# Eight experts on one core: weight pieces leave the branches, half of the first block's second layer goes into them, and small outputs move to a branch without matmuls

## The chip, the cores and the metric

The kernel runs on one core of one Trainium2 chip. Its engines are TensorE (PE, matmuls), VectorE (DVE), ScalarE (ACT), GpSimd (POOL) and SyncE (SP, which here only issues DMAs); each has its own instruction queue and runs it in order, and they wait for one another through semaphores. The metric is device time of the whole kernel in microseconds (us).

## The reference

Three parts follow each other. A chunked attention over 2 batches, 8 heads and 768 positions gives x of 1536 tokens by 512. A dense layer (512 to 2048 to 512, with a sigmoid gate) transforms x. Then a router takes, for each token, the best of 8 experts and gives it to that expert, up to a capacity of 384 tokens:

```
expert_idx = np.argmax(x @ w_gate, axis=1)
disp[e, counts[e]] = x[i]                      # tokens of expert e, in order
h = np.maximum(np.einsum('ecd,edf->ecf', disp, w1), 0.0)    # 512 -> 1024
y = np.einsum('ecf,efd->ecd', h, w2)                        # 1024 -> 512
out[i] = gate_w[i] * y[expert_idx[i], pos[i]]
```

The change touches the third part alone. With the inputs used, the experts have, in the order in which the kernel takes them (EORDER), 224, 291, 128, 160, 128, 256, 160 and 189 tokens. This text calls them the first to the eighth expert.

## The kernel before

Every float32 operand of a matmul is split into a high and a low part, and three products (high-high, high-low, low-high) stand for one. The tokens of an expert lie in blocks of 128. How many blocks an expert has is known only at run time, so the kernel branches on the count (tc.If, on every engine): a body of such a branch is called a leaf here.

The first layer (512 to 1024) has eight columns of 128 (fc). For one block (`first_of`) it is computed as two halves and transposed; for two blocks it is computed column by column (`first_of_two`, 12 matmuls per column); where the second block has at most 64 tokens, `first_of_narrow` computes a column with 8 matmuls, ACT and DVE make from it `low` and then `hT`, and POOL copies the second block's part of `hT` into `hp` (line 1084), two copies after all eight columns. The second layer (1024 to 512) of a block takes 24 matmuls of 512 columns (`layer2_part`, line 1003), that of a small block 16 (`small2`, line 941). Its result is scaled by the gate weight (ACT, line 1012; DVE, lines 944 and 945, for a small block) and scattered into the output by a POOL DMA (lines 1013 and 946).

Weights come as pieces, eight per expert (four of w1, four of w2), 512 KB each. SP loads a piece into one of eight raw buffers (line 241), ACT rounds it to its high part (line 295) and DVE subtracts that to get the low part (line 300). Six slots hold two pieces each. `w_next` moves the stream of pieces on by one; `steps(0)` brings it to the first three pieces of the next expert, `steps(1)` to all eight, which is possible when `w1_done` has given up the slots of the current first layer. So pieces 0 to 2 are made during the first layer of the expert before, and 3 to 7 behind it.

Before the change `steps(1)` stands inside every leaf, the second layer of the second block too, and all 24 matmuls of the first block's second layer come after the branches have met. Among these, an instruction (`hint`, lines 1191 and 1535) tells PE's sequencer which arm the next expert will probably take. The inputs take these leaves: the first expert its lone second block; the second expert two blocks and a third small one; the third and the fifth expert one block ("one"); the fourth, seventh and eighth the narrow leaf; the sixth two full blocks.

A scheduler orders the instructions of each engine within a block of the program; it doesn't move them over a branch. At the end of a leaf each engine's semaphore is brought to a common value.

## Time and profile before

| | us |
|---|---|
| median of three runs | 551.02 (548.78 to 552.99) |
| the profiled execution | 546.83 |
| its span | 545.0 |
| PE busy | 506.7 (93% of the span) |
| DVE, ACT, POOL busy | 316.3, 277.0, 117.4 |

The profiled execution lies 1.83 us above its span, and 0.8% below the median. The experts run from about 346 us to the end. A busy share is an average over the three parts; in the experts' part PE's idle times stand one by one in the timeline, each with what ended it. [...]

### The profile page before, as it was taken

The page shows a single profiled execution, that of the slowest core. Times are in us where ns is not written, and L with a number is a line of the kernel's source. Part 1 is how long each engine was busy: PE and PEld are TensorE (multiplying, and loading weights), DVE is VectorE, ACT ScalarE, POOL GpSimd, SP SyncE. Part 2 cuts the span into 40 slices and gives each one's busy share as a digit, 9 for nine tenths or more (in the row PEclk, how much of TensorE's full clock was granted, in tenths as well). Part 3 has the DMA queues.
Part 4 walks back from the last instruction along what each step waited for, and adds up shares of the span by engine and source line. Part 5 has one row for each costly group of instructions (what it writes and reads, how often), then busy time and mean ns, then how long its engine had stood idle before and what let it go on. Part 6 is the DMA issues. An engine that isn't in the chain of part 4 may idle for free.

```text
span 545.0 us, 10544 instructions
## 1 busy us (share of the span) xinstructions
PE 506.7 (93%) x4085; PEld 434.9 (80%) x4085; DVE 316.3 (58%) x633; ACT 277.0 (51%) x573; POOL 117.4 (22%) x113
## 2 busy tenths in 40 slices
PE   7899999999999999999999999978999499994985
PEld 3688889889999888999988887768887477984873
DVE  4999893687962652223373346293548918578231
ACT  2898877757632442222453334382637718666130
POOL 3335443334210220000000000630044133031201
PEclk9999999999999999999999999998999889998888
DMA  8887562043430022000285113797549938770100
GB/s 312 316 308 282 193 223 101 12 151 111 149 121 1 2 70 86 1 0 1 74 278 191 40 60 118 222 323 288 165 146 290 356 96 267 273 253 22 47 4 30
DMA packets 39163, 81.52 MB, mean 150 GB/s; under 512 B 3945, under 2 KB 10089, under 8 KB 39082
## 3 DMA queue, kind: packets, MB, share of 16 engines
q1 hardware_dynamic: 36010, 70.66, 37.5%
q0 software_dynamic: 3072, 9.80, 5.8%
q8 instruction: 48, 0.79, 0.6%
q14 instruction: 33, 0.27, 0.2%
HBM read 70.96 MB, written 9.75 MB: 148 GB/s over the span
## 4 chain that ended last, share of the span: by engine, by line
PE 70%; issue 8%; DMA 7%; DVE 6%; ACT 3%; POOL 1%; another core or an unknown queue 1%; SPq 1%; POOLq 0%; ACTq 0%; DVEq 0%
PE psh L547 25%; PE acc L590 25%; PE psy L1003 6%; DMA raw<-in_w_dram 4%; PE psh L879 3%; PE psy L941 3%; ACT w L295 3%; DVE w L300 2%; PE pse L505 2%; PE pss L435 1%; POOL hp L1084 1%; DMA kt<-in_k_dram 1%; DMA raw<-in_w_out_dram 1%; PE psr L615 1%
## 5 line engine op out<-in xcount | busy, mean ns | idle before, releaser
L547 PEld LDWEIGHTS psh<-xT,w 128*128 128x128 f32 x1152 | 147.0, 188 | 8.0 <-ACT g L566 0.3
L590 PE MATMUL acc<-w,g 128*128 128x512 f32 x576 | 153.0, 400 | 0.0
L547 PE MATMUL psh<-xT,w 128*128 128x256 f32 x1152 | 151.7, 281 | 0.0
L590 PEld LDWEIGHTS acc<-w,g 128*128 128x128 f32 x576 | 100.7, 188 | 19.4 <-issue 2.1
L562 ACT ACTIVATE sg<-psh 128x256 f32<-128x256 f32 x96 | 36.6, 383 | 126.1 <-PE psh L547 124.2
L300 DVE TENSOR_TENSOR w<-raw,w 128x1024 fp32r<-128x1024 f32 x64 | 76.4, 1221 | 28.3 <-ACT w L295 14.3
L570 DVE TENSOR_TENSOR g<-sg,g 128x256 fp32r<-128x256 f32 x78 | 38.2, 490 | 80.3 <-ACT g L566 77.7
L295 ACT ACTIVATE w<-raw 128x1024 fp32r<-128x1024 f32 x64 | 65.5, 1062 | 9.7 <-DMA raw<-in_w_dram 6.6
L1003 PE MATMUL psy<-w,hT 128*128 128x512 f32 x240 | 58.7, 398 | 0.8 <-DVE y L944 0.4
L1003 PEld LDWEIGHTS psy<-w,hT 128*128 128x128 f32 x240 | 44.4, 188 | 11.9 <-issue 1.1
L1012 ACT ACTIVATE y<-psy,gt 128x512 f32<-128x512 f32 x10 | 6.9, 689 | 60.7 <-PE psy L1003 55.9
L566 ACT ACTIVATE g<-psh 128x256 fp32r<-128x256 f32 x96 | 36.2, 379 | 0.0
L601 DVE SCALAR_TENSOR_TENSOR x<-acc,x 128x512 f32<-128x512 f32 x36 | 24.1, 686 | 20.8 <-PE acc L590 20.8
L827 POOL DMA_INDIRECT xr<-rows,taker x23 | 28.1, 1220 | 21.8 <-ACT w L295 6.8
L1069 PE MATMUL psh<-xs,w 128*128 128x384 f32 x96 | 28.8, 341 | 3.1 <-DVE low L1075 1.8
L879 PE MATMUL psh<-xs,w 128*128 128x256 f32 x192 | 25.4, 295 | 5.9 <-DVE w L300 3.2
L941 PE MATMUL psy<-w,hp 128*128 128x512 f32 x48 | 16.7, 520 | 15.2 <-POOL hp L1084 15.2
L879 PEld LDWEIGHTS psh<-xs,w 128*128 128x128 f32 x192 | 24.8, 201 | 6.9 <-issue 3.6
L725 POOL DMA_INDIRECT y<-rows,taker x1 | 1.2, 1213 | 123.8 <-DVE cnt_i L732 123.8
L941 PEld LDWEIGHTS psy<-w,hp 128*128 128x128 f32 x48 | 12.4, 264 | 19.0 <-POOL hp L1084 15.9
L1071 PE MATMUL psh<-xs,w 128*128 128x256 f32 x96 | 26.9, 280 | 0.0
L300 POOL TENSOR_TENSOR w<-w,w 128x512 fp32r<-128x512 f32 x12 | 16.7, 1400 | 42.8 <-ACT w L295 42.8
(163 smaller groups left out, 678.5 us busy)
## 6 DMA issues: line engine op xcount, KB each, us to landing
raw<-in_w_dram SPq DMA_DIRECT2D x64, 512.0 KB, 6.8
raw<-in_w_out_dram SPq DMA_DIRECT2D x16, 512.0 KB, 4.4
raw<-in_w_in_dram SPq DMA_DIRECT2D x16, 512.0 KB, 5.1
vt<-in_v_dram SPq DMA_DIRECT2D x12, 512.0 KB
kt<-in_k_dram SPq DMA_DIRECT2D x12, 368.0 KB, 5.3
qt<-in_q_dram SPq DMA_DIRECT2D x12, 256.0 KB, 6.2
out_dram<-blank SPq DMA_DIRECT2D x12, 256.0 KB, 2.6
rows<-x SPq DMA_DIRECT2D x5, 520.0 KB
```

Source lines behind the costliest of these rows:

```text
L295: nc.scalar.activation(out=w_dst(self.name, self.i, 0), in_=w, func=AF.Copy)
L300: eng.tensor_tensor(out=lo, in0=w, in1=hi.bitcast(F32), op=ALU.subtract)
L547: nc.tensor.matmul(ps, lhsT=w[:, wz, c, i * P:(i + 1) * P], rhs=xT[tb][:, xz, c, :], start=n == 0, stop=n == 3 * KC - 1)
L562: nc.scalar.activation(out=sg_t[u], in_=h_t[u], func=AF.Silu, scale=1.702)
L566: g_last[:1] = [nc.scalar.activation(out=g[:, 0], in_=h_t.pop(u), func=AF.Silu, scale=1.702).ins]
L570: lo = eng.tensor_tensor(out=g[:, 1], in0=sg_t.pop(u), in1=g[:, 0].bitcast(F32), op=ALU.subtract)
L590: nc.tensor.matmul(acc_t[tb][s], lhsT=g[:, gz, s * P:(s + 1) * P], rhs=w[:, wz, wi, :], start=i == 0 and n == 0, stop=u == last_of(k, tb) ...
L827: return nc.gpsimd.indirect_dma_start(out=t, out_offset=None, in_=rows[:, :], in_offset=bass.IndirectOffsetOnAxis(ap=taker[:, b, ex:ex + 1 ...
L879: mm = nc.tensor.matmul(ps, lhsT=w[:, wz, c, f0:f0 + P], rhs=t[:, xz, c, :], start=m == 0, stop=m == 3 * KC - 1)
L941: nc.tensor.matmul(ps, lhsT=h[:, fc].rearrange("p z n -> p (z n)"), rhs=w[:, wz, fc % 4, :], start=fc == 0 and wz == 0, stop=fc == F2 - 1 ...
L1003: nc.tensor.matmul(ps, lhsT=h[:, hz, fc, o:o + P], rhs=w[:, wz, fc % 4, :], start=fc == 0 and n == 0, stop=fc == F2 - 1 and n == 2)
L1069: nc.tensor.matmul(ps[:, :2 * n].rearrange("p (z n) -> p z n", z=2), lhsT=w[:, 0, c, f0:f0 + P], rhs=t[:, :, c, :n], start=c == 0, stop=False)
```

## The change

Inside the leaves no weight piece of the stream beyond `steps(0)` is left. Each leaf now ends with the first 12 matmuls (columns 0 to 3) of the first block's second layer (`head(0)`), behind the whole second layer of a second block. After the branches have met come `w1_done`, the other 12 matmuls (`tail(0)`), `steps(1)` and the gate; then a new branch on the count, which holds the scaling and the scatter of the second block (`send_second`) and no matmuls; then the first block's output. In the narrow leaf POOL copies into `hp` column by column, and the stream is moved once within the leaf (PUMPS_N) rather than three times. The hints are gone. The first expert has the same form with its blocks exchanged.

```diff
--- before.py
+++ after.py
@@ -33,6 +33,7 @@
 FROM = 150
 EV1 = 2
 PUMPS = (1, 3, 5)
+PUMPS_N = (4,)
 RAWS = 4
 RT = (4, 7)
 LOADS = 1000
@@ -41,7 +42,7 @@
 KEEP = 4
 KEEPS = (3, 8, 8)
 HALF = P // 2
-HEAD2 = 2
+HEAD2 = 4
 PUMPS1 = (0, 1, 1, 0)
 GFC = 2
 EORDER = (1, 2, 0, 3, 4, 5, 6, 7)
@@ -907,8 +908,6 @@
                 pv = ps[:, :KC * HALF].rearrange("p (c n) -> p c n", n=HALF)
                 nc.scalar.activation(out=x[:, :, 0], in_=pv, func=AF.Copy)
                 nc.vector.tensor_tensor(out=x[:, :, 1], in0=pv, in1=x[:, :, 0].bitcast(F32), op=ALU.subtract)
-                if e == 0:
-                    start2()
                 hs = []
                 for j in range(2):
                     w_tile(("w1", e, j), 0)
@@ -940,6 +939,9 @@
                 for wz in range(2):
                     nc.tensor.matmul(ps, lhsT=h[:, fc].rearrange("p z n -> p (z n)"), rhs=w[:, wz, fc % 4, :],
                                      start=fc == 0 and wz == 0, stop=fc == F2 - 1 and wz == 1)
+
+        def send_small(b):
+            ps = y_of(b)
             y = ep.tile([P, DM], F32, tag="y", name="y", bufs=2)[:HALF]
             nc.vector.tensor_scalar(out=y, in0=ps[HALF:], scalar1=gt[b][:HALF], scalar2=None, op0=ALU.mult)
             nc.vector.scalar_tensor_tensor(out=y, in0=ps[:HALF], scalar=gt[b][:HALF], in1=y, op0=ALU.mult, op1=ALU.add)
@@ -1002,10 +1004,6 @@
                 for n, (hz, wz) in enumerate(((0, 0), (0, 1), (1, 0))):
                     nc.tensor.matmul(ps, lhsT=h[:, hz, fc, o:o + P], rhs=w[:, wz, fc % 4, :],
                                      start=fc == 0 and n == 0, stop=fc == F2 - 1 and n == 2)
-
-        def layer2(b):
-            layer2_part(b, y_of(b), range(HEAD2 if e == 0 and b == 1 else 0, F2))
-            send(b)
 
         def send(b):
             y = ep.tile([P, DM], F32, tag="y", name="y", bufs=2)
@@ -1078,18 +1076,17 @@
                                                op0=ALU.max, op1=ALU.subtract)
                 if fc == TFC:
                     after_mm = mm.ins
-                if fc in PUMPS:
+                nc.gpsimd.tensor_copy(hT["pair"][:, fc], h[:, :, fc, P:n])
+                if fc in PUMPS_N:
                     w_next(e, KEEPS[0])
-            for z in range(2):
-                nc.gpsimd.tensor_copy(hT["pair"][:, :, z], hT_of(0)[:, z, :, P:P + HALF])
             with tc.issue_after(after_mm):
                 next_trans()
             steps(0)
 
-        def both(cond, yes, no, label=None):
+        def both(cond, yes, no):
 
             before = w_state()
-            with tc.If(cond, label=label) as some:
+            with tc.If(cond) as some:
                 yes()
             after = w_state()
             w_back(before)
@@ -1097,102 +1094,73 @@
                 no()
             assert w_state() == after
 
-        def start2():
-
-            layer2_part(1, y_of(1), range(HEAD2))
-
         def w1_done():
             for j in range(F // 512):
                 w_free(("w1", e, j))
 
-        def second_first():
-
-            w1_done()
-            steps(1)
-            layer2_part(1, y_of(1), range(HEAD2, F2 - 4))
-            parts[1].hint()
-            layer2_part(1, y_of(1), range(F2 - 4, F2))
-            send(1)
-
-        def third_first(b):
-
-            def go(is_wide):
-                if is_wide:
-                    trans(b, "h")
-                    start2()
-                    block_h(b)()
-                else:
-                    small_h(b)
-                second_first()
-                second_of(b, is_wide)
-
-            both(cnt[ex] > b * P + HALF, lambda: go(True), lambda: go(False))
-
-        def lone_second():
-            start2()
-            second_first()
-
-        def second_of(b, wide):
-
-            gate(b)
-            if wide:
-                layer2(b)
-            else:
-                small2(b)
-
-        def big():
-
-            both(cnt[ex] < P + HALF + 1, narrow_arm, wide)
-
-        def narrow_arm():
-
-            first_of_narrow()
-            w1_done()
-            steps(1)
-            second_of(1, False)
-
-        def wide():
-
-            first_of_two()
-            both(cnt[ex] < 2 * P + 1, two, third)
-
-        def two():
-
-            w1_done()
-            steps(1)
-            second_of(1, True)
-
-        def one():
-
-            first_of(0)
-            w1_done()
-            steps(1)
-
-        def third():
-
-            for b in range(2, NCB):
-                both(cnt[ex] > b * P + HALF, lambda: third_of(b, True), lambda: third_of(b, False))
-
-        def third_of(b, is_wide):
+        def head(b):
+
+            layer2_part(b, y_of(b), range(HEAD2))
+
+        def tail(b):
+
+            layer2_part(b, y_of(b), range(HEAD2, F2))
+
+        def third_first(b, is_wide):
 
             if is_wide:
                 trans(b, "h")
                 block_h(b)()
             else:
                 small_h(b)
-            two()
-            second_of(b, is_wide)
-
-        def hint():
-
-            traced = nc.cur_bb.bb.instructions
-            n = len(traced)
-            last = [i for i in traced if i.engine == mybir.EngineType.PE][-1].name
-            tc.mark_branch_hint_location(f"arms{e}", hint=cnt[ex] > P, engines=[mybir.EngineType.PE])
-            for i in traced[n:]:
-                tc.add_manual_dep(
-                    i, last, mybir.DependencyInfo(mybir.DependencyClass.NoSync, mybir.DependencyReason.DATA),
-                    reason="hint")
+
+        def third_second(b, is_wide):
+
+            gate(b)
+            if is_wide:
+                layer2_part(b, y_of(b), range(F2))
+                send(b)
+            else:
+                small2(b)
+                send_small(b)
+
+        def third(b, then):
+
+            def go(is_wide):
+                third_first(b, is_wide)
+                ys.pop(b, None)
+                third_second(b, is_wide)
+                then()
+
+            both(cnt[ex] > b * P + HALF, lambda: go(True), lambda: go(False))
+
+        def one():
+
+            first_of(0)
+            head(0)
+
+        def narrow_two():
+
+            first_of_narrow()
+            small2(1)
+            head(0)
+
+        def wide_two():
+
+            def then():
+                layer2_part(1, y_of(1), range(F2))
+                head(0)
+
+            first_of_two()
+            both(cnt[ex] < 2 * P + 1, then, lambda: third(2, then))
+
+        def send_second(wide):
+
+            gate(1)
+            if wide:
+                send(1)
+            else:
+                send_small(1)
 
         def after_first():
 
@@ -1212,25 +1180,31 @@
             y_of(1)
             hT_of(2)
             xs_of(2)
-            both(cnt[ex] < 2 * P + 1, lone_second, lambda: third_first(2))
+            both(cnt[ex] < 2 * P + 1, lambda: head(1), lambda: third(2, lambda: head(1)))
+            w1_done()
+            steps(1)
+            tail(1)
+            send(1)
 
         def others():
 
             assert NCB == 3
-            y_of(1)
+            for b in range(2):
+                y_of(b)
             for b in range(2, NCB):
                 load(b)
                 hT_of(b)
                 xs_of(b)
-            both(cnt[ex] > P, big, one, label=f"arms{e}")
+            both(cnt[ex] > P, lambda: both(cnt[ex] < P + HALF + 1, narrow_two, wide_two), one)
+            w1_done()
+            tail(0)
+            steps(1)
             gate(0)
-            layer2_part(0, y_of(0), range(1))
-            if e + 1 < E:
-                parts[e + 1].hint()
-            layer2_part(0, y_of(0), range(1, F2))
+            with tc.If(cnt[ex] > P):
+                both(cnt[ex] > P + HALF, lambda: send_second(True), lambda: send_second(False))
             send(0)
 
-        return SimpleNamespace(hint=hint, adopt=adopt, load=load, trans=trans, xs_of=xs_of, after_first=after_first, others=others,
+        return SimpleNamespace(adopt=adopt, load=load, trans=trans, xs_of=xs_of, after_first=after_first, others=others,
                                before_arms=before_arms)
```

How this moves instructions is shown at three places. SP at the end of the first expert's leaf (the lone second block) and behind it; raw_0_3362 to raw_3_3365 and raw_0_4523 to raw_3_4526 are the eight raw buffers. Before:

```order
L1092 COMPARE_AND_BRANCH
L241 DMA raw_3_3365<-in_w_dram 128x2x512
L241 DMA raw_0_4523<-in_w_dram 128x2x512
L241 DMA raw_1_4524<-in_w_dram 128x2x512
L241 DMA raw_2_4525<-in_w_dram 128x2x512
L241 DMA raw_3_4526<-in_w_dram 128x2x512
L1092 UNCONDITIONAL_BRANCH
```

(where the leaves have met, one load of raw_2_3364 follows, ahead of the second expert's arms). Now:

```order
L1089 UNCONDITIONAL_BRANCH x2
L242 DMA raw_2_3364<-in_w_dram 128x2x512
L242 DMA raw_0_4523<-in_w_dram 128x2x512
L242 DMA raw_1_4524<-in_w_dram 128x2x512
L242 DMA raw_2_4525<-in_w_dram 128x2x512
L242 DMA raw_3_4526<-in_w_dram 128x2x512
L242 DMA raw_3_3365<-in_w_dram 128x2x512
L1089 COMPARE_AND_BRANCH x2
```

The leaf has no load any more; raw_2_3364 is loaded first behind it, ahead of the five others.

PE in the fourth expert, the end of the narrow leaf (psy is the sum of a second layer, hp the second block's first-layer result, hT that of the first block, w_95 and w_1723 the slots of w2), and its meeting point. Before:

```order
L846 MATMUL pst<-ident,xr 128x128 x8
L941 MATMUL psy<-w_95,hp 128x512 x8
L941 MATMUL psy<-w_1723,hp 128x512 x8
L1092 UNCONDITIONAL_BRANCH
...
L1003 MATMUL psy<-w_95,hT 128x512 x3
L1191 REGISTER_ALU
L1535 BRANCH_PREFETCH_HINT
L1003 MATMUL psy<-w_95,hT 128x512 x9
L1003 MATMUL psy<-w_1723,hT 128x512 x12
L1092 COMPARE_AND_BRANCH x2
```

Now:

```order
L847 MATMUL pst<-ident,xr 128x128 x8
L940 MATMUL psy<-w_95,hp 128x512 x8
L940 MATMUL psy<-w_1723,hp 128x512 x8
L1005 MATMUL psy<-w_95,hT 128x512 x12
L1089 UNCONDITIONAL_BRANCH
...
L1005 MATMUL psy<-w_1723,hT 128x512
L1203 COMPARE_AND_BRANCH
L1089 COMPARE_AND_BRANCH
L1089 UNCONDITIONAL_BRANCH x2
L1203 UNCONDITIONAL_BRANCH
L1005 MATMUL psy<-w_1723,hT 128x512 x11
L1089 COMPARE_AND_BRANCH x2
```

Twelve of the 24 matmuls now stand in the leaf; one matmul, the new branch and eleven matmuls stand behind it, and the hint is gone.

DVE from the end of the third expert's leaf ("one") into the fourth expert's narrow leaf; each L300 or L301 row makes the low part of one piece, the slots w_95, w_1723, w_96 and w_4519 say which. Before:

```order
L300 TENSOR_TENSOR w_95<-raw_1_4524,w_95 128x1024
L300 TENSOR_TENSOR w_1723<-raw_2_4525,w_1723 128x1024
L300 TENSOR_TENSOR w_1723<-raw_3_4526,w_1723 128x1024
L1092 UNCONDITIONAL_BRANCH
L858 TENSOR_SCALAR gs<-gs 128x1
L859 RECIPROCAL gt<-gs 128x1
L1092 COMPARE_AND_BRANCH x2
L300 TENSOR_TENSOR w_94<-raw_0_3362,w_94 128x1024
L300 TENSOR_TENSOR w_94<-raw_1_3363,w_94 128x1024
L1075 TENSOR_TENSOR low<-psh,low 128x192 x2
```

Now:

```order
L1089 UNCONDITIONAL_BRANCH
L301 TENSOR_TENSOR w_95<-raw_0_4523,w_95 128x1024
L301 TENSOR_TENSOR w_95<-raw_1_4524,w_95 128x1024
L301 TENSOR_TENSOR w_1723<-raw_2_4525,w_1723 128x1024
L301 TENSOR_TENSOR w_1723<-raw_3_4526,w_1723 128x1024
...
L1203 UNCONDITIONAL_BRANCH
L301 TENSOR_TENSOR w_4519<-raw_3_3365,w_4519 128x1024
L1089 COMPARE_AND_BRANCH x2
L301 TENSOR_TENSOR w_94<-raw_0_3362,w_94 128x1024
L301 TENSOR_TENSOR w_94<-raw_1_3363,w_94 128x1024
L1073 TENSOR_TENSOR low<-psh,low 128x192 x2
```

Five pieces have left the leaf: four stand where the leaves have met, ahead of the new branch, and the piece left over from the next expert's w1 stands behind it; so seven pieces lie between the leaf's end and the first `low` of the fourth expert, where two were.

## Rows read from the trace of the kernel before

**Rows 1.** The page, busy time of the engines:

```profile
PE 506.7 (93%) x4085; PEld 434.9 (80%) x4085; DVE 316.3 (58%) x633; ACT 277.0 (51%) x573; POOL 117.4 (22%) x113
```

**Rows 2.** PE, timeline of the second expert: start, us, work, [idle before, releaser]:

```profile
366.45 8.88 PE L879 MATMUL psh<-xs,w 128*128 128x256 f32 x60 [3.20 <-DVE w L300]
377.00 4.60 PE L879 MATMUL psh<-xs,w 128*128 128x256 f32 x36 [1.67 <-DVE hT L883]
```

**Rows 3.** Stretches: length, busy us of each engine (instructions), granted clock, DMA share, GB/s:

```profile
366.45:381.44 14.99, 13.32 (x96) 13.12 (x97) 5.95 (x10) 3.42 (x9) 1.90 (x1) 0.89 0.81 285
502.95:508.72 5.77, 5.77 (x16) 4.59 (x17) 0.00 (x0) 0.00 (x0) 0.00 (x0) 0.63 0.03 6
526.64:532.00 5.36, 5.36 (x16) 4.25 (x17) 0.00 (x0) 0.00 (x0) 0.00 (x0) 0.68 0.03 6
368.00:370.00 2.00, 2.00 (x12) 2.00 (x11) 1.00 (x2) 0.38 (x1) 0.35 (x1) 0.50 0.96 332
```

**Rows 4.** DVE, timeline ahead of the second expert's start:

```profile
359.41 9.16 DVE L300 TENSOR_TENSOR w<-raw,w 128x1024 fp32r<-128x1024 f32 x8
```

**Rows 5.** The chain of waits into the second expert, its last step:

```profile
366.92 8.22 DMA raw<-in_w_dram
```

**Rows 6.** PE, timeline of the sixth expert (both layers):

```profile
461.85 11.67 PE L879 MATMUL psh<-xs,w 128*128 128x256 f32 x95 [1.06 <-DVE gs L858]
474.15 11.32 PE L1003 MATMUL psy<-w,hT 128*128 128x512 f32 x48
```

**Rows 7.** PE, timeline of the third and fourth expert:

```profile
394.13 3.90 PE L941 MATMUL psy<-w,hT 128*128 128x512 f32 x16
...
403.47 1.79 PE L963 MATMUL psh<-w,xs 128*128 128x512 f32 x7
...
417.96 0.41 PE L1069 MATMUL psh<-xs,w 128*128 128x384 f32 x1 [1.29 <-DVE gs L858]
...
426.44 0.45 PE L1069 MATMUL psh<-xs,w 128*128 128x384 f32 x1 [1.05 <-DVE low L1075]
...
436.14 5.27 PE L941 MATMUL psy<-w,hp 128*128 128x512 f32 x16 [6.26 <-POOL hp L1084]
441.77 5.85 PE L1003 MATMUL psy<-w,hT 128*128 128x512 f32 x24 [0.35 <-issue]
```

**Rows 8.** DVE, timeline: the third expert's last pieces, the fourth's last columns:

```profile
413.19 4.62 DVE L300 TENSOR_TENSOR w<-raw,w 128x1024 fp32r<-128x1024 f32 x4
...
433.45 1.03 DVE L1077 SCALAR_TENSOR_TENSOR hT<-low,hT 128x192 fp32r<-128x192 f32 x2
```

**Rows 9.** POOL, timeline, the fourth expert's second copy into hp:

```profile
434.54 1.54 POOL L1084 CAST hp<-hT 128x512 fp32r<-128x512 f32 x1 [0.28 <-DVE hT L1077]
```

**Rows 10.** PE, timeline of the seventh and eighth expert:

```profile
493.25 0.44 PE L1069 MATMUL psh<-xs,w 128*128 128x384 f32 x1 [0.77 <-DVE low L1075]
...
502.95 5.93 PE L941 MATMUL psy<-w,hp 128*128 128x512 f32 x16 [6.25 <-POOL hp L1084]
...
526.64 5.54 PE L941 MATMUL psy<-w,hp 128*128 128x512 f32 x16 [2.68 <-POOL hp L1084]
...
533.02 5.69 PE L1003 MATMUL psy<-w,hT 128*128 128x512 f32 x22 [0.38 <-DVE y L944]
```

**Rows 11.** DVE, timeline, the eighth expert's last column and its second block's output:

```profile
525.20 0.36 DVE L1077 SCALAR_TENSOR_TENSOR hT<-low,hT 128x192 fp32r<-128x192 f32 x1 [0.43 <-ACT hT L1076]
532.22 0.75 DVE L944 TENSOR_SCALAR y<-psy,gt 64x512 f32<-64x512 f32 x1 [6.66 <-PE psy L941]
```

**Rows 12.** The chain that ended last, a step of its end:

```profile
534.02 2.83 DMA out_dram<-y,taker
```

**Rows 13.** The page: ACT's half of a piece; weight loads; one instruction queue:

```profile
L295 ACT ACTIVATE w<-raw 128x1024 fp32r<-128x1024 f32 x64 | 65.5, 1062 | 9.7 <-DMA raw<-in_w_dram 6.6
...
raw<-in_w_dram SPq DMA_DIRECT2D x64, 512.0 KB, 6.8
...
q8 instruction: 48, 0.79, 0.6%
```

## The prediction, made before the changed kernel ran

> **What bounds the kernel now.** I read the page first, then PE's timeline through the experts, then the chain of waits where PE stands idle. PE is busy for 93% of the span [rows 1], so the experts are worth reading gap by gap: only an idle time of PE, or a stretch in which PE runs slowly, can be won. Five places count. The second expert starts after 3.20 us of idle time that ended with a DVE weight piece [rows 2]: DVE was still making the pieces of the first expert's leaf, eight in 9.16 us [rows 4], and PE needs none of the last five. The same expert's first layer takes 14.99 us at a mean clock of 0.89, with 0.50 early in it [rows 3] and a stall of 1.67 [rows 2]; the sixth expert's, of the same shape, takes 11.67 [rows 6]. The narrow leaves wait 6.26, 6.25 and 2.68 us for POOL's `hp` copies [rows 7, 10]. Their 16 small matmuls then run slowly: 5.27, 5.77 and 5.36 us [rows 7, 3], where the same 16 took 3.90 in the second expert [rows 7], because the clock in these stretches was 0.63 and 0.68 [rows 3], after idle times of 6.25 and 2.68. Small gaps stand at three meeting points: 1.29 and 1.06 behind DVE's gate, 0.35 and 0.38 behind the leaf [rows 7, 6, 10].
>
> **The change, part by part.** Times are us against the profiled 546.83.
>
> Second expert. The five pieces leave the first expert's leaf, so the 3.20 goes. The load of raw_2 was issued at 366.92 and took 8.22 [rows 5], behind those five loads on SP; now it waits only for its own buffer, which DVE finishes five pieces earlier, 5 x 1.15 = 5.7 us [rows 4], so near 361. It then lands near 369, about when PE has run through its free sums (five columns of 11.67 / 8 = 1.46). So the first layer should take the sixth expert's time: 14.99 - 11.67 = 3.32 saved. I take off 1.1 for what is late next, the fifth column's wait and fewer filling matmuls in the small third block (bounds 0 and 3.3). **-5.4.**
>
> Third expert ("one"). PE reaches the end of the leaf after half the second layer. 24 matmuls are 24 x 0.236 = 5.7 us (11.32 / 48, [rows 6]); PE ended at 417.96 - 1.29 = 416.67, so the half ends at 413.8. DVE ends the leaf's last piece at 413.19 + 1.15 = 414.35 [rows 8]. The meeting point joins both: **+0.55.**
>
> Fourth expert (narrow). The 1.29 goes, since the gate no longer follows the last piece. But seven pieces now stand ahead of its first `low` on DVE where two did. PE starts it near 417.4 (414.35, twelve matmuls 2.8, branches 0.2) and comes to its fifth column, which needs the first sum's bank back, 4 x 1.24 later, at 422.4 (six columns lie between 417.96 and the wait at 426.44, [rows 7]). DVE needs until 414.35 + 7 x 1.15 = 422.4 for the pieces alone, and the gate and `low` come on top: a gap of under 1 at the least. Where DVE also waits once or twice for ACT's halves (1.06 each) or for a load (6.8 from its issue, [rows 13]), it is up to 3. I take 2.0, against 1.05 before [rows 7]: +0.95. The clock stayed up after 1.29 idle and fell after 2.68, so I charge half of 1.4: +0.7. The copies per column leave only the last of eight behind the last `hT`. It costs about 0.4 (a quarter of 1.54, [rows 9]) and lies beside the first small matmuls, which need the earlier columns; in the eighth expert the last `hT` ended at 525.56 [rows 11], 1.6 after PE's first layer, and the seven pairs of matmuls ahead of it take 3.4. So the 6.26 goes, and with it 5.27 - 3.90 = 1.37 and 0.35; +0.2 for a first copy that is late. -1.29 + 0.95 + 0.7 - 6.26 - 1.37 - 0.35 + 0.2 = **-7.4.**
>
> Fifth and sixth expert: the same join, +0.55; the 1.06 goes; the same backlog, but a wide column takes 0.22 more than a narrow one, four of them 0.9, so a gap of 1.1: **+0.6.**
>
> Seventh expert: 6.25 goes, 5.77 - 3.90 = 1.87 of slow clock too; pieces 3, 0 and 1 ahead of the first `low` give a gap of 1.1 for 0.77 [rows 10], +0.2 for the copy: **-7.6.** The long leaf of the sixth expert hides pieces 4 to 7; without that cover it would be the second rival.
>
> Eighth expert: 2.68, 5.36 - 3.90 = 1.46 and 0.38 go; no pieces follow: **-4.5.**
>
> End. The first block's scatter must follow the second's, which takes 2.83 after its issue [rows 12]. Before, the second's was out at 534.02, near five us ahead of PE's end. Now its two DVE steps (0.75 each, [rows 11]) follow the leaf, whose end lies 2.8 ahead of PE's end: 2.8 cover all but 1.5 of 1.5 + 2.83, and the first block's own scaling half of that. **+0.8** (0 to 2).
>
> Branches. Behind one matmul PE meets the new branch, at seven experts. The trace shows 0 (row 474.15 follows a branch without a gap, [rows 6]) to 0.35 and 0.38 for a meeting point [rows 7, 10]; I take 0.2, nearer the middle as more jumps stand here: **+1.4** (0 to 2.7). [...] No row here times a branch alone. The hints are gone: at the two experts that take the "one" leaf, the farthest jump, 0.4 each by the 0.38, **+0.8** (0 to 2 x 6.8, the nearest DMA row from above).
>
> Removing the pieces' stream steps from the narrow columns (two of three) costs nothing: the same pieces are made later, and counted above.
>
> Sum: -5.4 + 0.55 - 7.4 + 0.6 - 7.6 - 4.5 + 0.8 + 1.4 + 0.8 = -20.8, so 526.0 for the profiled execution. The median of the runs lies 0.77% above it (551.02 / 546.83), so 530.
>
> **Rivals.** First, slower: **PE waits for its instructions.** The far jumps, leaf to meeting point and meeting point to the next arms, lose their hint and have 12 and 11 matmuls in front, 2.8 and 2.6 us of cover. Instructions do come by DMA (48 transfers on one queue, [rows 13]); a DMA took from 2.83 [rows 12] to 6.8 [rows 13] here. With 2.83 the cover holds; with 5.0 it lacks 2.2 and 2.4, 4.6 per expert, 32 over seven: 546.83 - 20.8 + 32 = 558, 562 as a median. It decides from about 4.7 us: then it eats 20.8 and 5.5 more. Against it: unhinted leaf ends before cost 0.35, 0.38 or nothing, though with 16 or 24 matmuls ahead of them. [...] 6%.
>
> Second, **the pieces start only where the leaves meet for every engine**, as PE before waited for DVE's leaf end [rows 2]. Then pieces 4 to 7 aren't hidden by the leaves of the fourth, sixth and seventh expert either. With four pieces (4.6), the gate, the branch and three or one more pieces behind the leaf's end, the waits inside the fifth, seventh and eighth expert grow by 1.2, 2.0 and 1.5, the slow clock returns in two of them (1.4 each), and the full gap of 3 stays in the fourth and sixth (1.0 and 1.0): +9.5, 535.5, a median of 540. 20%.
>
> Third, better: **the backlog is hidden and the jumps cost nothing.** Without 0.95, 0.7, 1.1, 0.33, 2.2, 0.8: 6.1 less, 520, a median of 524. 13%.
>
> Fourth, the gains are found but are given back to loads: the experts from the second to the fourth draw 285 to 332 GB/s at DMA shares of 0.81 to 0.96 [rows 3], and a stream that starts later in each expert can't catch up. If each of the first three gives back its 4 to 5 us, 14 in all: 540, a median of 544; with more, no change. 6%.
>
> **How the numbers follow.** My forecast has 55%. A change of 1%, 5.5 us, is about what a measurement of this kernel tells from none. Forecast and third rival, most of the second and half of the fourth lie below 545.5: 0.86 faster; 0.08 within 1%; 0.06 slower. The range goes from the third rival with the lowest of the runs' spread (524 - 2) to the second and the fourth: 522 to 544.
>
> **What would show it.** Right: no idle time at the second expert's start, none or under 1 us ahead of the small matmuls of the narrow leaves, these at 3.9 us, and waits of 1 to 3 us for `low` at the fifth column of the fourth, sixth and seventh experts. Wrong: idle time of PE's sequencer at the jumps (the chain would say issue or PEq), or a granted clock under 0.8 in the new leaves.

## The result and the profile after

The changed kernel takes 531.43 us (median of four runs, 530.1 to 537.04) against 551.06 beside it: a ratio of 0.9665, with a 95% interval of 0.9586 to 0.9743. Forecast were 530, and 522 to 544. The profiled execution has 531.93 us and a span of 530.1, 14.9 less than before.

PE's timeline through the experts, in the order of the second to the eighth; columns as in [rows 2]:

```profile
364.67 11.69 PE L880 MATMUL psh<-xs,w 128*128 128x256 f32 x96 [0.82 <-DVE w L301]
...
403.47 0.51 PE L965 MATMUL psh<-w,xs 128*128 128x512 f32 x1 [0.90 <-issue]
...
420.73 0.59 PE L1067 MATMUL psh<-xs,w 128*128 128x384 f32 x1 [3.45 <-DVE low L1073]
...
427.80 3.98 PE L940 MATMUL psy<-w,hp 128*128 128x512 f32 x16
...
431.62 5.76 PE L1005 MATMUL psy<-w,hT 128*128 128x512 f32 x24
...
441.74 5.79 PE L965 MATMUL psh<-w,xs 128*128 128x512 f32 x18 [4.36 <-issue]
...
456.08 5.86 PE L880 MATMUL psh<-xs,w 128*128 128x256 f32 x48
...
464.35 7.48 PE L880 MATMUL psh<-xs,w 128*128 128x256 f32 x48 [2.40 <-DVE hT L884]
...
489.59 0.45 PE L1067 MATMUL psh<-xs,w 128*128 128x384 f32 x1 [0.98 <-DVE low L1073]
...
495.35 3.98 PE L940 MATMUL psy<-w,hp 128*128 128x512 f32 x16
...
518.00 5.73 PE L1005 MATMUL psy<-w,hT 128*128 128x512 f32 x24
```

The second expert starts after 0.82 us of idle time where [rows 2] had 3.20, and its first layer runs through in 11.69, the sixth expert's 11.67 of [rows 6]. The small matmuls of the narrow leaves (L940) follow without a wait and take 3.98 where [rows 7, 10] had 5.27 and 5.93 behind 6.26 and 6.25. Three waits are new or longer. The fifth column of the fourth expert waits 3.45 for `low` (1.05 before, [rows 7]), that of the sixth 2.40, and ahead of the fifth expert PE stands idle for 4.36 us with nothing that the profile shows to wait for; 18 matmuls behind it take 5.79 where 18 x 0.236 would be 4.25. The sixth expert's last four columns take 7.48 behind their wait, its first four 5.86.

Stretches of the same kernel, columns as in [rows 3]:

```profile
364.67:376.36 11.69, 11.69 (x98) 11.69 (x99) 8.76 (x13) 6.46 (x12) 2.01 (x1) 1.00 1.03 368
...
420.73:427.01 6.28, 6.28 (x33) 6.28 (x33) 4.83 (x13) 3.65 (x12) 1.71 (x6) 0.73 1.03 387
...
427.80:431.62 3.82, 3.82 (x19) 3.09 (x18) 3.41 (x6) 3.82 (x8) 1.12 (x3) 1.00 0.11 36
...
437.38:441.74 4.36, 0.00 (x1) 0.04 (x1) 1.23 (x1) 1.63 (x2) 1.94 (x2) 0.95 1.02 366
```

Granted clocks are shares of full speed; the traces of both kernels have only 1.00 and 0.50, and a value between them is a mean over a stretch. The second expert's first layer has the full clock (1.00), the fourth expert's last four columns behind the wait of 3.45 have 0.73, the small matmuls 1.00. The sixth expert's last four columns have 0.77, the 18 matmuls behind the idle 4.36 us 0.74. In the idle time of 4.36 the DMA engines are full: share 1.02, 366 GB/s.

By segments, from one expert's first matmul to the next one's, worked out from the two timelines:

| expert | before | after | difference | forecast |
|---|---|---|---|---|
| up to the second's start, second | 16.80 + 37.02 | 14.42 + 33.71 | -5.7 | -5.4 |
| third and fourth | 43.98 | 43.36 | -0.6 | -6.9 |
| fifth and sixth | 37.85 | 42.11 | +4.3 | +0.6 |
| seventh | 29.01 | 20.95 | -8.1 | -7.6 |
| eighth | 24.40 | 18.93 | -5.5 | -4.5 |
| end | 6.29 | 6.37 | +0.1 | +0.8 |

The forecast's branches and hints (+2.2) lie across the rows. The profiles begin the experts at slightly different times (after: 0.6 later), which belongs to nothing in the change.

### The profile page after: what moved, and what is told of

The parts are those of the page before. It is cut to its first block, busy times and chain, and to the rows that moved or that the text cites. A ratio compares the mean times of both kernels' runs of the same rounds, so it can differ in the third digit from the quotient of the medians.

```text
span 530.1 us, 10682 instructions
## 1 busy us (share of the span) xinstructions
PE 503.4 (95%) x4081; PEld 435.3 (82%) x4085; DVE 317.6 (60%) x633; ACT 279.3 (53%) x573; POOL 125.3 (24%) x131
## 5 line engine op out<-in xcount | busy, mean ns | idle before, releaser
L301 DVE TENSOR_TENSOR w<-raw,w 128x1024 fp32r<-128x1024 f32 x64 | 75.5, 1221 | 29.7 <-ACT w L296 27.2
L828 POOL DMA_INDIRECT xr<-rows,taker x23 | 33.6, 1463 | 39.9 <-PE psy L1005 15.2
L1067 PE MATMUL psh<-xs,w 128*128 128x384 f32 x96 | 30.1, 352 | 4.4 <-DVE low L1073 4.4
L301 POOL TENSOR_TENSOR w<-w,w 128x512 fp32r<-128x512 f32 x12 | 16.7, 1400 | 42.7 <-ACT w L296 42.7
L291 POOL TENSOR_TENSOR w<-w,rest 128x512 int32<-128x512 int32 x13 | 17.6, 1355 | 35.4 <-DVE w L277 29.2
L965 PE MATMUL psh<-w,xs 128*128 128x512 f32 x72 | 20.1, 427 | 6.2 <-issue 5.3
L266 ACT ACTIVATE w<-raw 128x512 f32<-128x512 f32 x32 | 21.3, 675 | 8.1 <-DMA raw<-in_w_out_dram 6.6
```

The lines of the kernel that those rows point to most:

```text
L301: eng.tensor_tensor(out=lo, in0=w, in1=hi.bitcast(F32), op=ALU.subtract)
L828: return nc.gpsimd.indirect_dma_start(out=t, out_offset=None, in_=rows[:, :], in_offset=bass.IndirectOffsetOnAxis(ap=taker[:, b, ex:ex + 1 ...
L965: nc.tensor.matmul(p1[j], lhsT=x[:, xz, c, o:o + P], rhs=w[:, wz, c, :], start=(xz, wz, c) == (0, 0, 0), stop=(xz, wz, c) == (1, 0, KC - 1))
L1067: nc.tensor.matmul(ps[:, :2 * n].rearrange("p (z n) -> p z n", z=2), lhsT=w[:, 0, c, f0:f0 + P], rhs=t[:, :, c, :n], start=c == 0, stop=False)
```

## The experiments

Times are medians; the kernel before took 549.3 to 550.4 beside them, and the changed kernel, run again beside the last three, 533.07 (ratio 0.9713, 0.9665 to 0.976). Of that second run stood on record:

> The changed kernel itself, run beside the next three so that they can be compared with it: 531 by either theory, 0.966 of before.

### What the idle 4.36 us are

**The hints put back** (behind the first column, three matmuls, after the meeting point, in the changed kernel):

```diff
-            tail(0)
+            layer2_part(0, y_of(0), range(HEAD2, HEAD2 + 1))
+            parts[e + 1].hint()
+            layer2_part(0, y_of(0), range(HEAD2 + 1, F2))
```

> The changed kernel with the hints put back behind the first matmul after each meeting point; nothing else. Theory A (PE waits for the instructions of the far arm, which the removed hint would have fetched): the 4.36 us of idle time ahead of the fifth expert and the 0.90 inside the third go, and with the first the slow clock behind it (18 matmuls in 5.79 us for 4.36): 5 to 7 us less than the changed kernel, about 525. Theory B (PE waits there for something that the profile doesn't show, a semaphore or a load): the gap stays and the time is within 1 us of 531.4.

539.19 us, ratio 0.9796 (0.9746 to 0.9845). PE ahead of the fifth expert:

```profile
447.26 5.97 PE L965 MATMUL psh<-w,xs 128*128 128x512 f32 x18 [4.64 <-issue]
```

The stall stays, so theory A's expectation fell; but theory B, no change, did not hold either, since the time rose by 6 to 8 us in small waits at other places. PE's sequencer runs ahead of its matmuls (by 2.84 us at the branch shown below): by the trace this hint stood only 0.15 us ahead of its branch (439.63 and 439.78), in the kernel before 1.40 us (441.89 and 443.29). That the hints gained anything there is not shown.

**The leaf for one block first:**

```diff
-            both(cnt[ex] > P, lambda: both(cnt[ex] < P + HALF + 1, narrow_two, wide_two), one)
+            both(cnt[ex] < P + 1, one, lambda: both(cnt[ex] < P + HALF + 1, narrow_two, wide_two))
```

> The changed kernel with the outer branch turned round: the leaf for one block stands first, behind it the narrow and the wide ones; no instruction of a leaf changes. Theory A (the 4.36 us of idle time ahead of the fifth expert and the 0.90 inside the third are PE waiting for the instructions of the leaf that stood last, a long jump away): both go, with them the slow clock behind the first, 5 to 7 us less than the changed kernel, about 525; the narrow and wide leaves begin after a short jump and wait under 1 us. Theory B (every taken jump costs a fetch, the distance doesn't matter): the stall moves to the fourth, sixth, seventh and eighth expert and the time rises, 535 to 545. Theory C (PE waits for something else): no change, 531.

530.33 us, ratio 0.9654 (0.9629 to 0.968). PE:

```profile
371.48 4.77 PE L880 MATMUL psh<-xs,w 128*128 128x256 f32 x38 [2.83 <-issue]
...
424.64 0.45 PE L1067 MATMUL psh<-xs,w 128*128 128x384 f32 x1 [0.96 <-DVE low L1073]
...
440.01 4.35 PE L965 MATMUL psh<-w,xs 128*128 128x512 f32 x18
...
457.57 2.79 PE L880 MATMUL psh<-xs,w 128*128 128x256 f32 x16 [2.94 <-ACT w L296]
```

The order of leaves alone takes the stall away: the fifth expert starts at 440.01 behind the fourth's last matmul, and its 18 matmuls take 4.35. A stall of 2.83 appears in the second expert's wide leaf, which now lies farther off, two columns into it. So the idle time belongs to the place of the instructions, as A says, and it is partly moved, as B says. The 2.94 ahead of the sixth expert, and a wait of 2.16 in the third, are put down to ACT by the profile; but PE's own branch ended after ACT's piece at both (457.41 after 457.27, 414.48 after 414.42), so they are moved stalls too. The DMA queues in the 4.36 us of the changed kernel (columns: packets, MB, share of the 16 engines):

```profile
q1 hardware_dynamic: 569, 1.08, 66.7%
q0 software_dynamic: 159, 0.47, 31.8%
q14 instruction: 3, 0.02, 1.8%
q8 instruction: 1, 0.02, 1.5%
```

The profile calls q8 and q14 instruction queues; their four packets, 0.04 MB, came here among 1.1 MB of weight pieces and 0.5 MB of gathered and scattered rows. What PE did meanwhile stands in the row of its own branch (PEldq is PE's sequencer; shortest, median and longest in ns, then the start):

```profile
L1089 PEldq COMPARE_BRANCH  x1: 7030/7030/7030, 434.5 to 434.5; - x1
```

The branch to the fifth expert's leaf begins at 434.54 and takes 7.03. PE is still busy for 2.84 of it with the matmuls in its queue, and the next matmul starts 0.17 behind the branch's end: 7.03 - 2.84 + 0.17 = 4.36. So the whole stall is PE's own jump, and no other engine holds it. In the fourteen runs 100 of PE's branches from 345 us on take over 1.5 us, and in each a 16 KB packet of q8 landed 1.2 to 2.5 us ahead of the branch's end, which points to q8 as the queue that brings PE's instructions. The 0.90 inside the third expert and the 2.83 above stand behind no branch; there too a packet of q8 landed 1.6 us ahead of the next instruction.

**Half the matmuls at the leaf's end:**

```diff
-HEAD2 = 4
+HEAD2 = 2
```

> The changed kernel with HEAD2 = 2: 6 of the first block's 24 matmuls at the end of a leaf and 18 behind the meeting point, in place of 12 and 12. Theory A (queued matmuls hide the fetch behind a jump): the stall ahead of the fifth expert shrinks by the six matmuls, 1.4 us, from 4.36 to about 3, while stalls of 1 to 2 us show at the narrow leaves' ends, whose cover falls from 2.8 to 1.4 us: in all 0 to 6 us more. Theory B (the stall isn't a fetch): both stay, within 1 us of 531.4.

535.57 us, ratio 0.975 (0.9714 to 0.9785). PE at the fourth expert's meeting point and ahead of the fifth:

```profile
434.28 0.49 PE L1005 MATMUL psy<-w,hT 128*128 128x512 f32 x1 [0.74 <-ACT w L296]
...
443.36 6.54 PE L965 MATMUL psh<-w,xs 128*128 128x512 f32 x18 [4.17 <-issue]
```

The total went as A expected, the places did not: the stall ahead of the fifth expert shrank by 0.2, not 1.4, though six more matmuls stood before it, and the narrow leaves' ends cost 0.6 to 0.9 each. The six did cover 1.3 more (4.14 for 2.84), but the branch itself took 8.14 for 7.03.

### What the parts of the change are worth

**Copies by column alone** (with one step of the weight stream in the narrow leaf for three), in the kernel before:

```diff
-                if fc in PUMPS:
+                nc.gpsimd.tensor_copy(hT["pair"][:, fc], h[:, :, fc, P:n])
+                if fc in PUMPS_N:
                     w_next(e, KEEPS[0])
-            for z in range(2):
-                nc.gpsimd.tensor_copy(hT["pair"][:, :, z], hT_of(0)[:, z, :, P:P + HALF])
```

> The kernel before with one part of the change: POOL copies column by column and one step of the weight stream in a narrow leaf. Theory A (the waits for hp come from POOL's two copies after all columns): the waits of 6.26, 6.25 and 2.68 fall to 1 to 2 us and the small matmuls' clock recovers: 12 to 15 us less than before, about 537. Theory B (they come from the weight pieces which the leaf lets into the columns' chain on ACT and DVE): the first two waits stay above 4 us, only the eighth expert's goes: 4 to 7 us less.

549.7 us, ratio 0.9992 (0.9955 to 1.0029): nothing. PE in the fourth expert:

```profile
436.16 0.73 PE L942 MATMUL psy<-w,hp 128*128 128x512 f32 x2 [1.17 <-POOL hp L1082]
...
437.39 0.73 PE L942 MATMUL psy<-w,hp 128*128 128x512 f32 x2 [0.50 <-POOL hp L1082]
...
440.99 7.23 PE L1004 MATMUL psy<-w,hT 128*128 128x512 f32 x24 [2.87 <-issue]
```

The wait for hp shrinks to 1.17 and 0.50, as A said. But behind the leaf's last small matmul PE now stands idle for 2.87, and the 24 matmuls after it take 7.23 for 5.85. The same comes at the seventh (2.83) and the eighth (1.71). PE's branch at the end of this leaf, here and in the kernel before:

```profile
L1092 PEldq COMPARE_BRANCH  x1: 3550/3550/3550, 437.4 to 437.4; - x1
...
L1092 PEldq COMPARE_BRANCH  x1: 5496/5496/5496, 436.2 to 436.2; - x1
```

The jump was there before too, and longer. It began when the old wait of 6.26 was over, with all 16 small matmuls still to run: they covered 5.20 of its 5.50, and 0.35 of idle time showed. With copies by column the small matmuls run as their columns come, and when the sequencer reaches the branch PE has 0.73 left to do.

**Pieces 3 to 7 out of the leaves alone**, in the kernel before:

```diff
             first_of_narrow()
-            w1_done()
-            steps(1)
...
             both(cnt[ex] > P, big, one, label=f"arms{e}")
+            w1_done()
+            steps(1)
             gate(0)
```

> The kernel before with one part of the change: pieces 3 to 7 move from the leaves to behind the meeting point; second layers, outputs and hints stay. Theory A (the pieces in the leaf cost the 3.20 at the second expert and, in the narrow leaves, all of the hp wait above the eighth expert's 2.68): second expert 5.4 less, narrow leaves 3.5 less twice: about 10 to 12 us less than before. Theory B (pieces 4 to 7 now stand behind the second block's output, which DVE makes after the small second layer, so the next expert's columns wait): what is gained in the leaf is lost at the next expert, 3 to 6 us less or nothing.

551.61 us, ratio 1.0047 (1.0015 to 1.0078): no gain. PE in the third and fourth experts:

```profile
411.84 0.66 PE L846 MATMUL pst<-ident,xr 128*128 128x128 f32 x4 [4.06 <-DMA xr<-rows,taker]
...
427.16 0.45 PE L1069 MATMUL psh<-xs,w 128*128 128x384 f32 x1 [2.48 <-DVE low L1075]
...
435.93 4.38 PE L941 MATMUL psy<-w,hp 128*128 128x512 f32 x11 [2.84 <-POOL hp L1084]
```

The hp wait falls to 2.84, the column wait rises to 2.48 as theory B said. The third expert waits 4.06 for its rows, a gather that both theories had missed.

**The pieces back in the leaves of the changed kernel** (the first expert's stay out):

```diff
             first_of_narrow()
+            w1_done()
+            steps(1)
             small2(1)
```

> The changed kernel with the weight pieces 3 to 7 put back into the leaves of all experts but the first; copies by column, the matmuls at the leaf's end and the new branch stay. Theory A (the fetch behind the jump is slow since the loads that SP issues at the meeting point fill the DMA engines, share 1.02): with the loads in the leaf the stall ahead of the fifth expert falls below 1.5 us, the waits for the fifth column fall to those of before (about 1), and the hp waits come back at 1 to 2 us in two narrow leaves: 526 to 533. Theory B (the pieces in the leaf are what cost the time in the narrow leaves): 538 to 545.

533.8 us, ratio 0.9695 (0.9648 to 0.9743). PE at the fourth expert's meeting point and the fifth's start:

```profile
435.85 0.49 PE L1005 MATMUL psy<-w,hT 128*128 128x512 f32 x1 [2.23 <-issue]
...
441.60 4.42 PE L965 MATMUL psh<-w,xs 128*128 128x512 f32 x18 [1.10 <-issue]
```

No difference from the changed kernel that this can tell: the stall ahead of the fifth expert fell to 1.10, as A expected, but 2.23 came behind the leaf, and 1.81 behind the seventh's.

**The second block's output back in its leaf:**

```diff
             small2(1)
+            send_second(False)
             head(0)
...
-            with tc.If(cnt[ex] > P):
-                both(cnt[ex] > P + HALF, lambda: send_second(True), lambda: send_second(False))
```

> The changed kernel without the new branch: the second block's gate, scaling and scatter stand in its leaf, between its second layer and the first block's 12 matmuls. Theory A (the new branch frees DVE: in the leaf its scaling waits for the small second layer, and pieces 4 to 7 queue behind it): the fifth, seventh and eighth experts wait 1 to 3 us longer in all, some 2 to 6 us more than the changed kernel. Theory B (the branch itself costs PE 0.2 us at seven experts, and DVE has time): 1 to 2 us less.

534.37 us, ratio 0.9723 (0.9687 to 0.9758). PE:

```profile
423.57 0.69 PE L1067 MATMUL psh<-xs,w 128*128 128x384 f32 x1 [3.32 <-DVE low L1073]
...
441.57 4.43 PE L965 MATMUL psh<-w,xs 128*128 128x512 f32 x18 [1.47 <-issue]
...
491.33 0.44 PE L1067 MATMUL psh<-xs,w 128*128 128x384 f32 x1 [2.57 <-DVE low L1073]
```

The seventh expert's column waits 2.57 for 0.98, as A said; against that the stall ahead of the fifth expert is 1.47 for 4.36. Two waits for gathered rows came besides, 1.83 and 2.33. In all not to be told from the changed kernel.

**Both of these together:** pieces and outputs in the leaves, so that of the change the column copies, the missing hints, the first expert's pieces and the 12 matmuls at the leaf's end are left.

> The changed kernel with pieces 3 to 7 back in the leaves (but the first expert's) and the second block's output too, so that only the column copies, the missing hints and the 12 matmuls at the leaf's end are left of the change. Theory A (those 12 matmuls give the gain, since they hide the fetch behind the leaf's jump, which cost 2.87 and 2.83 us and a slow clock in the run with the copies alone): 535 to 540. Theory B (pieces and outputs must leave the leaf too, or PE waits for DVE at the meeting point): 541 to 549.

527.99 us, ratio 0.961 (0.9574 to 0.9646), the fastest of all, some 5 below the changed kernel beside it. PE, from the second expert to the fifth's start:

```profile
365.27 11.69 PE L880 MATMUL psh<-xs,w 128*128 128x256 f32 x96 [0.40 <-DVE w L301]
...
413.24 0.41 PE L1067 MATMUL psh<-xs,w 128*128 128x384 f32 x1 [1.27 <-DVE gs L859]
...
421.42 0.45 PE L1067 MATMUL psh<-xs,w 128*128 128x384 f32 x1 [0.75 <-DVE low L1073]
...
434.18 4.61 PE L1005 MATMUL psy<-w,hT 128*128 128x512 f32 x12 [1.96 <-issue]
...
439.44 4.42 PE L965 MATMUL psh<-w,xs 128*128 128x512 f32 x18 [0.65 <-PE psy L1005]
```

The column wait is 0.75, the fifth expert starts after 0.65, and behind the narrow leaf 1.96 are left. Theory A held, with more than it expected. Against the copies alone (549.7) that is 22 us; 5 to 6 of them are the second expert's (0.40 and 11.69 here, 3.20 and a slow clock there). The 12 matmuls were not run by themselves; that most of the rest is theirs follows from the jumps that they cover, not from a run of its own.

**The jump to the fifth expert in all these kernels.** Each row is read from PE's branch and the stretch that it takes:

| kernel | branch, us | PE busy in it | DMA share in it | idle time |
|---|---|---|---|---|
| before | 3.47 | 3.47 | 0.18 | 0 |
| changed | 7.03 | 2.84 | 0.96 | 4.36 |
| hints put back | 7.31 | 2.84 | 0.96 | 4.64 |
| half the matmuls at the leaf's end | 8.14 | 4.14 | 0.97 | 4.17 |
| pieces back in the leaves | 4.85 | 3.92 | 0.33 | 1.10 |
| output back in its leaf | 4.69 | 3.39 | 0.48 | 1.47 |
| both | 5.03 | 4.55 | 0.58 | 0.65 |

The idle time is what PE's queued matmuls leave of the branch. The branch is long where the DMA engines are full; since these kernels differ in more than their loads, that the loads lengthen it is likely, not shown.

### The wait for the fifth column

Timelines of the changed kernel between the third and the fourth expert, ACT first, then DVE:

```profile
415.24 0.69 ACT L1010 ACTIVATE y<-psy,gt 128x512 f32<-128x512 f32 x1 [2.32 <-DVEq L1203]
...
415.83 2.94 ACT L296 ACTIVATE w<-raw 128x1024 fp32r<-128x1024 f32 x3
```

```profile
409.02 5.79 DVE L301 TENSOR_TENSOR w<-raw,w 128x1024 fp32r<-128x1024 f32 x5
...
416.91 3.50 DVE L301 TENSOR_TENSOR w<-raw,w 128x1024 fp32r<-128x1024 f32 x3 [1.83 <-ACT w L296]
```

PE ended the third expert near 412.4, but ACT could scale its output only at 415.24, when DVE had made its five pieces (409.02 to 414.8) and, behind them, the gate that ACT scales by (414.92); three pieces on both engines follow, then `low`. Two kernels move this. **The output ahead of the new branch, behind an early gate:**

```diff
-            steps(1)
             gate(0)
+            steps(1)
+            if e + 1 < E:
+                send(0)
             with tc.If(cnt[ex] > P):
```

> The changed kernel with the gate ahead of the weight pieces and the first block's output ahead of the new branch (in all experts but the last). Theory A (the 3.45 and 2.40 us waits for the fifth column arise since ACT's output of the first block waits for DVE behind pieces 4 to 7, and three pieces queue behind that output): the output moves to PE's end, 412.4 in place of 415.2, DVE becomes the limit, the waits fall to about 2.0 and 1.0 and the clock in the fourth expert stays up: 3 to 6 us less. Theory B (DVE's seven pieces alone set the wait, the output's place is hidden): the waits stay within 0.5 us and so does the time.

536.95 us, ratio 0.977 (0.9708 to 0.9831), slower than the changed kernel. PE:

```profile
403.06 7.12 PE L965 MATMUL psh<-w,xs 128*128 128x512 f32 x18 [3.25 <-issue]
...
425.48 0.45 PE L1067 MATMUL psh<-xs,w 128*128 128x384 f32 x1 [1.99 <-DVE low L1073]
...
468.14 2.05 PE L880 MATMUL psh<-xs,w 128*128 128x256 f32 x15 [1.09 <-DVE hT L884]
```

The two waits fell to 1.99 and 1.09, as A expected to a tenth. The time was lost where neither theory looked: the third expert now starts after a stall of 3.25 at its jump (PE's branch takes 6.90 for 4.31), 18 matmuls take 7.12, and the seventh expert's wait rises from 0.98 to 2.95. With the leaf for one block first as well:

> The leaf for one block first (as in the run of that name) and the first block's output ahead of the new branch with an early gate. Theory A (with the long jump gone, the earlier output can now show its gain, which in its own run was lost to a longer fetch in the third expert): the waits of 0.96 in the fourth and 2.94 in the sixth expert fall to 0 to 1, 2 to 4 us less than 530.3. Theory B (the waits behind the meeting points are now set by fetches of ACT and DVE, which run into the same jumps): within 1.5 us of 530, or more.

534.02 us, ratio 0.9715 (0.9675 to 0.9755), the changed kernel's 0.9713: theory B, or more. **The next expert's fourth piece in the leaf** (KEEPS = (4, 8, 8)):

> The changed kernel with KEEPS = (4, 8, 8): the next expert's fourth piece is made in the leaf too, not behind the output of the first block. Theory A (the waits for the fifth column come from the number of pieces between the output and the first column on ACT and DVE): two pieces in place of three, the waits fall by 1.2 us each, 3.45 to 2.2, 2.40 to 1.2 and 0.98 to 0; the meeting points wait up to 1.2 longer for DVE in two leaves: 0 to 3 us less than the changed kernel. Theory B (ACT waits in the leaf for that piece's load): the columns of the second expert stall behind it, 1 to 4 us more.

533.27 us, ratio 0.9697 (0.966 to 0.9734). The fourth expert's column and the fifth's start:

```profile
423.72 0.44 PE L1067 MATMUL psh<-xs,w 128*128 128x384 f32 x1 [3.38 <-DVE low L1073]
...
444.31 5.03 PE L965 MATMUL psh<-w,xs 128*128 128x512 f32 x11 [4.38 <-issue]
```

The wait stays at 3.38 for 3.45: two pieces follow the output in place of three, but the output itself waits for one more. A piece moved from behind the output to ahead of it gains nothing, and theory A fell; the output moved ahead of the pieces, in the run before, had taken 1.46 off.

## Why the prediction was right, and where not

The forecast of 530 met 531.43, but the profiled execution was to be 526.0 and was 531.93; the median of the changed kernel did not lie 0.77% above it, as I had assumed from the kernel before. That hides a miss of 6 us: from the third to the sixth expert the change gave 10 less than forecast, elsewhere 4 more. That the two misses and the 0.77% left the median within 2 us of the forecast is luck. Of the signs named beforehand both kinds showed: 0.82 at the second expert, small matmuls at 3.98 without a wait and waits of 3.45, 2.40 and 0.98 on the one side, idle time put down to issue at a jump (4.36) and a clock of 0.73 in a leaf on the other.

- *Second expert, -5.4:* right (-5.7), by the steps given: 0.82 idle, first layer 11.69. Of the 0.82, 0.6 is PE's own branch, which ended at 364.45.
- *Narrow leaves:* the waits and the slow clock of the small matmuls went, and seventh and eighth experts gained 8.1 and 5.5 for 7.6 and 4.5. What the sum lacked is why: the copies alone gain nothing. The 12 matmuls at the leaf's end count, as cover for the jump (3.50 at the fourth expert's leaf end, PE busy all through it); in the sum I had priced them at nothing.
- *Backlog:* the mechanism was right (the run with the output moved shows it), the size too small: 3.45 for 2.0, above the bound of 3, and 2.40 for 1.1. Behind each, four columns ran slowly: 6.28 for 4 x 1.24, so 1.3 where I had 0.7, and in the sixth expert 7.48 for 5.86, 1.6 where I had nothing. The join at the meeting point, +0.55 twice, shows no idle time.
- *Branches and hints, +2.2:* the new branch cost PE nothing that shows as idle time in the seventh and eighth experts. The step "the hints are gone: at the two experts that take the "one" leaf, the farthest jump, 0.4 each" failed: at the fifth expert it was 4.36, and 1.5 more in the 18 matmuls behind it (the 0.90 in the third stands behind no branch). The missing hints did not make it, since 4.64 stayed with them. It is the first rival's mechanism at one jump: a branch of 7.03, where the rival had reckoned with 5.0, over 2.84 of cover. PE's other long branches took 1.6 to 4.3 and were hidden but for 0.6 and 0.15. My counter-evidence did not hold: the leaf end that cost 0.35 was a jump of 5.50 beside 5.20 of slow matmuls, and the 0.38 was a wait for DVE [rows 10]. The trace does time branches alone: 0.18 and 0.24 for the two ahead of the branch of 7.03. The stalls of 4.36 and 2.87 are each PE's branch, of 7.03 and 3.55, with a packet of q8 inside.
- *End, +0.8:* 0.1; the chain's last scatter was out in time:

```profile
520.00 3.27 DMA out_dram<-y,taker
```

- *Second rival:* its place was right for the fourth and sixth experts, at about half its price; the fifth, seventh and eighth stayed free of it. *Fourth rival:* the loads did not stop the second expert, whose first layer ran at share 1.03.

Still open: how much the weight loads add to PE's jumps. With the DMA engines nearly idle (shares 0.03 and 0.02) the branches at the seventh and eighth leaves' ends took 3.53 and 3.29 in the changed kernel. No run changed the loads alone.

## What to carry to other kernels

Ahead of a far jump, look in the trace for the engine's own branch and for the work that is queued when it begins: 5.2 us at the fourth expert's leaf end before, 0.73 there with the copies alone, 2.84 at the stall of 4.36. Ask what work a wait just ahead of a jump holds back: with the copies alone the wait of 6.26 shrank to 1.17 and 0.50, only 0.73 of the small matmuls ran beside the jump, and 2.87 of idle time came in the wait's place; with 12 matmuls put there, in the changed kernel, none showed at that jump. Parts of a change that give nothing when timed one by one can still give all of it together; here two of the parts (the pieces and the outputs out of the leaves) cost 5 us together, and only the run without them showed it.

## What was unexpected of the hardware

Which of two leaves stands first in the program took a 4.36 us stall of PE from one expert and put stalls of 2.83, 2.16 and 2.94 us into three others. And a run that only moved the gate and the output, with no matmul moved, changed the idle time at a jump of PE from 0.15 to 3.25 us.
